# Merged first transfers, products by kind, other banks for one FFT stage and a shared last eviction in a one-core attention and spectral-filter kernel

## The chip, the cores and the metric

The kernel runs on one core of one Trainium2 chip. The metric is the device time of one execution, in microseconds (us). The core has a matrix engine (TensorE, "PE"; its weight loads are listed as "PEld"), a vector engine (VectorE, "DVE"), a scalar engine (ScalarE, "ACT"), GpSimd ("POOL") and SyncE ("SP"), which here only issues transfers. PE writes into eight accumulator banks of 128 x 512 float32 each; DVE and ACT read them. Engines work each in its own order of instructions and wait for one another through semaphores.

## The reference

Two independent halves, side by side in the output of shape (1, 2048, 896). The first is attention with 16 query heads of 28 and one key and value head shared by all of them; the second a spectral filter: a two-dimensional real FFT over 2048 x 448, a product with complex weights, and the inverse.

```python
q = (x @ wq).reshape(B, S, H, Dh).transpose(0, 2, 1, 3)   # S=2048, H=16, Dh=28, D=448
k = x @ wk
v = x @ wv
p = softmax(einsum("bhqd,bkd->bhqk", q, k) * Dh**-0.5)
a = einsum("bhqk,bkd->bhqd", p, v).transpose(0, 2, 1, 3).reshape(B, S, H * Dh) @ wo
X = rfft2(x2, axes=(-2, -1)) * (w_r + 1j * w_i)           # x2: a second (1, 2048, 448) input
b = irfft2(X, s=(S, D), axes=(-2, -1))
out = concatenate([a, b], axis=-1)
```

## The kernel before

*Precision.* Products of the attention's linear maps are made of float32 numbers split in a high and a low part: `xh` and `xl` for the input, `wqh` and `wql` for the weights. Three products (high by high, low weight by high input, high weight by low input) are summed in one bank.

*Phase 1, projections.* The sequence is cut in four column chunks `c` of 512. The outputs (queries of 16 heads, keys and values, 512 rows padded) are four groups `g` of 128. The contraction over 448 is cut in four quarters `j`; the last holds 64 rows, stacked twice so that its high and low parts share one product. `split_w` (L257) and `split_x` (L264) make the parts from tiles called `raw`: ACT casts the weights, DVE subtracts; for chunk 0 the inputs' cast is DVE's, later ACT's. `proj` (L275 to L279) issues the products of one group and quarter, `evac` (L281 to L285) copies a finished bank to `qraw` with ACT and takes its largest absolute value with DVE into `qmx`. Chunk 0 runs quarter by quarter over all four groups (L304 to L309), because its inputs arrive from memory meanwhile; chunks 1 to 3 group by group (L327 on). Twenty products of zeros (L229 to L234) run ahead of the first transfer's landing.

*Input transfers.* SP's queue brings `xa` (the input, transposed) in quarters of 128 x 512 and the weights `wq` in quarters of the same size, alternately, each into a `raw` tile of eight buffers; the first weight quarter comes in two pieces of 128 and 384 columns. POOL's queue brings two small key rows (`krow`) into `kf` at the start (L196, L197).

*The FFT along the width, interleaved.* After six of the twelve groups of chunks 1 to 3 (`places`, L287), one eighth `q` of the second input is worked on: `fft1_load` (L86) brings it in, `fft1_fold` (L95 to L108) adds and subtracts on DVE in ten operations, `fft1_a` (L121) multiplies on PE, ACT copies the result out (L124), `fft1_mm` (L136) multiplies again into banks 6 and 7, and `fft1_out` copies those out, with ACT (L145) for q below 6 and DVE (L147) for 6 and 7, and stores them. All other products of phase 1 take banks 0 to 5 in turn (`spin`).

*Keys and bound.* `fetch` gathers the rows of keys and values from `qraw` into `kf` by transfers; `keys(0)` casts the first half to `ka` with ACT (L206) and subtracts with DVE (`kl`, L210). `key_max` takes the largest key value over the maxima of the first groups (`qm`, L296), and PE spreads it (L299); `terms` and `shift` make from it, per head, a bound on the scores (L216 to L221), and `build_q` (L166) the shifted queries. At the handoff (L369 to L431) the last FFT eighths, 16 small transposes of values (L388), `fft1_mm(6)` (L390) and a branch on the bound (L393, L394) follow one another.

*Phase 2, attention.* For each of the 16 pairs of chunk and group, 16 key blocks, and four heads there is a score product (L810, 1024 in all), an exponential (ACT, L827, with 20 buffers for results), and value products into bank 7 (L840). Between them go the second FFT stages, the filter and the output map `wo` (L739).

*What sets the order.* PE's order is the program's own everywhere. For DVE, ACT, SP and POOL, up to L436, a scheduler places instructions by its own cost model among those whose inputs it expects to be ready. From L436 on all engines follow the program, and there a planner decides it when the kernel is built: a clock per engine (`clk`, L442), a time at which each bank comes free (`free`, L443), queues of fill work (`fill`), `score` (L806), `exps`, `values` (L833) and `first_fill` (L852, the product set `fft1_mm(7)`). A score takes the bank that is free first; `first_fill` comes when no bank is free for the first time.

*The tail.* Four products (L955) add the last group's share to four banks, and `wo_out` copies each out with ACT (L744) and stores it from ACT's queue (L749).

Of the kernel before, what the change touches and what calls it, by code (L numbers as in the profile page):

```python
# [12 lines left out]
F32 = mybir.dt.float32  # L13
# [3 lines left out]
AF = mybir.ActivationFunctionType  # L17
# [5 lines left out]
S, D, H = 2048, 448, 16  # L23
# [10 lines left out]
WARM = 10, 10  # L34
# [3 lines left out]
def kernel(ctx: ExitStack, tc: tile.TileContext, t: dict):  # L38
# [90 lines left out]
    def fft1_mm(q):  # L129
        w = xb[q][1]  # L130
        pb = view(bank[6], 2, 226), view(bank[7], 2, 226)
        for p in range(2):
            a = at1.pop((q, p))
            for h in range(2):
                for e in range(2):
                    mm(pb[h][64 * e:64 * e + 64, p], w[64 * h:64 * h + 64, 2 * p + e], a[64 * h:64 * h + 64, e],  # L136
                       start=True, stop=True)
        return pb
# [48 lines left out]
    with tc.tile_pool(name="f1", bufs=2) as f1[0], tc.tile_pool(name="w1", bufs=1) as w1:  # L187
# [8 lines left out]
        nc.gpsimd.dma_start(kf[DH:DH + 1], t["krow"][0:1])  # L196
        nc.gpsimd.dma_start(kf[32 + DH:64], t["krow"][1:5])  # L197
# [26 lines left out]
        with tc.tile_pool(name="x1", bufs=2) as x1:  # L224
# [11 lines left out]
            def raw(src, eng):  # L236
                r = x1.tile([128, 512], F32, name="raw", bufs=8)
                eng.dma_start(r, src)
                return r


            first = slice(0, 128), slice(128, 512)
            xr, wr = {}, {}
            xr[0, 0] = raw(t["xa"][0, :, 0], nc.sync)
            wr[0] = x1.tile([128, 512], F32, name="raw", bufs=8)
            for s in first:
                nc.sync.dma_start(wr[0][:, s], t["wq"][:, 0, s])
            for j in range(1, NK):
                xr[0, j] = raw(t["xa"][0, :, j], nc.sync)
                wr[j] = raw(t["wq"][:, j], nc.sync)  # L250

# [23 lines left out]
            def proj(pq, xh, xl, g, j):  # L275
                gs = slice(g * 128, (g + 1) * 128)
                parts = ((wqh, xh), (wql, xh), (wqh, xl)) if j < 3 else ((wqh, xh), (wql, xh))
                for n, (w, x) in enumerate(parts):
                    mm(pq, w[:, j, gs], x[:, j], start=(j == 0 and n == 0), stop=(j == 3 and n == 1))  # L279
# [24 lines left out]
            for j in range(NK):  # L304
                split_x(*xs[0], 0, j)
                split_w(j)
                for g in range(NG):
                    proj(pqs[g], *xs[0], g, j)
                xr[1, j] = raw(t["xa"][1, :, j], nc.sync)  # L309
            fft1_consts()  # L310
            fft1_load(0)
            parts_of(1)
            for j in range(NK):
                split_x(*xs[1], 1, j)
                xr[2, j] = raw(t["xa"][2, :, j], nc.sync)
# [11 lines left out]
            for c in range(1, NC):  # L327
                for g in range(NG):
# [4 lines left out]
                    if g == 0 and c < 3:  # L333
                        parts_of(c + 1)
                        for j in range(NK):
                            split_x(*xs[c + 1], c + 1, j)
                            if c < 2:
                                xr[c + 2, j] = raw(t["xa"][c + 2, :, j], nc.sync)
# [51 lines left out]
        pb6 = fft1_mm(6)  # L390
# [52 lines left out]
    free = [0.0] * 6 + [2.0]  # L443
# [297 lines left out]
    def wo_out(p, c, k, on_act=False):  # L741
        if on_act:
            y = pp.tile([128, D], F32, name="yb", tag="p")
            nc.scalar.activation(y, p, AF.Copy)  # L744
        else:
            y = ap.tile([128, D], F32, name="ya")
            V.tensor_copy(y, p)  # L747
        r0 = c * CW + k * 128
        (nc.scalar if on_act else nc.sync).dma_start(t["oa"][r0:r0 + 128], y)  # L749
# [204 lines left out]
    for k in range(4):  # L954
        mm(tail[k], o[:, 128 * k:128 * k + 128], w3, start=False, stop=True)  # L955
        wo_out(tail[k], c, k, True)
# [55 lines left out]
def _layout(A_x, A_wq, A_wk, A_wv, A_wo, B_x, B_w_r, B_w_i):  # L1012
# [3 lines left out]
    z["xa"] = xt.reshape(NK, 128, NC, CW).transpose(2, 1, 0, 3)  # L1016
# [4 lines left out]
    z["wq"] = wq.reshape(D, 512)[rows].reshape(NK, 128, 512).transpose(1, 0, 2)  # L1021
# [51 lines left out]
```

## Time and profile before

| | us |
|---|---|
| Median of 3 runs | 644.1 (643.01 to 645.8) |
| Profiled execution, its own time | 643.85 |
| Profiled execution, span | 642.1 |
| PE busy | 633.9 |
| ACT busy | 548.0 |
| DVE busy | 333.4 |

The span runs from the first to the last instruction or transfer that the profiler saw; the execution's own time is a little longer. Times in rows of the timeline count from the span's start. A row gives start, length, engine, line, operation, output <- inputs and the tile's shape, and in brackets the idle time ahead of it with what ended it; "xN" folds several instructions into one row. Phase 1 lasts until about 72 us, the attention until about 627, the tail until the end.

### The profile page before, as it was taken

The numbers are of one execution on the slowest core, as the hardware profiler recorded it, in microseconds if no ns is written. First come the engines' busy times: TensorE is split into PE (matmuls) and PEld (weight loads), VectorE is DVE, ScalarE is ACT, GpSimd is POOL, SyncE is SP. The second block draws the span as 40 slices with busy tenths as digits, with TensorE's granted clock in tenths as the row PEclk, the third lists the DMA queues.
The fourth block names the chain that finished last, engine by engine and source line by source line (L and its number), as shares of the span: only waits on it lengthen the run. The fifth ranks groups of instructions, "written<-read, shape, count | busy, mean of one in ns | idle before, by whom it ended". The sixth has DMA issues, their size and how long they took to land.

```text
span 642.1 us, 11693 instructions
## 1 busy us (share of the span) xinstructions
PE 633.9 (99%) x4384; PEld 359.1 (56%) x4384; DVE 333.4 (52%) x685; ACT 548.0 (85%) x1101; POOL 91.2 (14%) x170
## 2 busy tenths in 40 slices
PE   8999999999999999999999999999999999999997
PEld 6877544444444455554445655655665665564444
DVE  6999612499898987896821411315323510321003
ACT  4544799999999997889999879878988888889991
POOL 2021031201021201020132020010211101020200
PEclk9999899999999999999999999999999999999999
DMA  8756499512133321131692332232425131131001
GB/s 275 262 150 181 113 241 211 140 26 59 44 100 87 114 67 32 38 76 28 163 240 64 99 78 69 63 79 83 120 77 142 47 81 47 38 90 44 19 1 58
DMA packets 31162, 63.35 MB, mean 99 GB/s; under 512 B 7093, under 2 KB 18918, under 8 KB 29884
## 3 DMA queue, kind: packets, MB, share of 16 engines
q1 hardware_dynamic: 23168, 39.98, 23.3%
q0 software_dynamic: 7360, 21.69, 12.6%
q10 hardware_dynamic: 576, 0.92, 0.4%
q8 instruction: 35, 0.57, 0.4%
q14 instruction: 23, 0.19, 0.1%
HBM read 30.56 MB, written 15.02 MB: 71 GB/s over the span
## 4 chain that ended last, share of the span: by engine, by line
PE 88%; ACT 0%; ACTq 0%; DVE 0%; issue 0%; DVEq 0%
PE b L810 41%; PE b L840 36%; PE b L739 6%; PE b L680 2%; PE b L661 2%; PE b L136 0%; ACT yb L744 0%; ACTq L749 0%; PE b L955 0%; DVE bs L147 0%; ACTq L393 0%; ACT bs L145 0%; DVEq L147 0%; ACTq L744 0%
## 5 line engine op out<-in xcount | busy, mean ns | idle before, releaser
L827 ACT ACTIVATE p<-b 128x512 f32<-128x512 f32 x1024 | 506.6, 777 | 48.1 <-PE b L810 46.9
L810 PE MATMUL b<-qa,ka 128*128 128x512 f32 x1024 | 284.3, 411 | 0.4 <-DVE bs L147 0.4
L810 PEld LDWEIGHTS b<-qa,ka 128*128 128x128 f32 x1024 | 182.7, 189 | 126.0 <-ACT p L827 82.3
L840 PE MATMUL b<-p,vs 128*32 128x512 f32 x2048 | 240.0, 597 | 0.0
L840 PEld LDWEIGHTS b<-p,vs 128*32 128x32 f32 x2048 | 56.5, 109 | 121.7 <-issue 120.3
L710 POOL DMA_DIRECT2D sd<-qraw x15 | 8.8, 589 | 260.0 <-DVE qraw L705 260.0
L705 DVE COPY qraw<-b 128x512 f32<-128x512 f32 x15 | 10.4, 692 | 65.6 <-PE b L840 65.6
L747 DVE COPY ya<-b 128x448 f32<-128x448 f32 x12 | 7.5, 625 | 56.9 <-PE b L739 54.7
L719 POOL DMA_DIRECT2D R<-rd x60 | 29.9, 504 | 42.4 <-DMA rd<-rs 30.3
L544 DVE SCALAR_TENSOR_TENSOR X<-w,X 128x226 f32<-128x226 f32 (+2 forms) x72 | 34.0, 473 | 2.4
L667 DVE COPY X<-b 113x512 f32<-113x512 f32 (+1 forms) x16 | 11.1, 692 | 34.1 <-ACT p L827 28.7
L685 DVE COPY X<-b 128x226 f32<-128x226 f32 x16 | 6.3, 392 | 41.4 <-ACT p L827 38.5
L279 PE MATMUL b<-xh,wqh 128*128 128x512 f32 x64 | 25.8, 403 | 0.9 <-ACT wqh L261 0.9
L283 ACT ACTIVATE qraw<-b 128x512 f32<-128x512 f32 x16 | 9.2, 600 | 19.0 <-PE b L279 19.0
L279 PE MATMUL b<-xh,wql 128*128 128x512 f32 x64 | 25.1, 392 | 0.1
L739 PE MATMUL b<-woh,oh 128*128 128x448 f32 x60 | 22.1, 368 | 0.0
L739 PE MATMUL b<-wol,oh 128*128 128x448 f32 x60 | 22.1, 368 | 0.0
L739 PE MATMUL b<-woh,ol 128*128 128x448 f32 x60 | 22.0, 366 | 0.0
L279 PE MATMUL b<-xl,wqh 128*128 128x512 f32 x48 | 18.8, 391 | 0.0
L727 DVE TENSOR_TENSOR qraw<-qraw,R 128x512 f32<-128x512 f32 x15 | 10.3, 685 | 14.7 <-DMA R<-rd 14.7
L680 PEld LDWEIGHTS b<-cs,X 113*128 113x128 f32 (+1 forms) x128 | 16.8, 191 | 1.4
L537 DVE SCALAR_TENSOR_TENSOR w<-X 128x113 f32<-128x113 f32 (+2 forms) x56 | 17.5, 352 | 0.1
(108 smaller groups left out, 515.9 us busy)
## 6 DMA issues: line engine op xcount, KB each, us to landing
qa<-qa SPq DMA_DIRECT2D x15, 512.0 KB, 4.2
X<-t POOLq DMA_DIRECT2D x16, 452.0 KB, 6.5
wf<-w POOLq DMA_DIRECT2D x10, 452.0 KB, 4.6
raw<-xa SPq DMA_DIRECT2D x16, 256.0 KB, 5.0
xb<-xb SPq DMA_DIRECT2D x8, 512.0 KB, 3.6
qa<-qh SPq DMA_DIRECT2D x60, 64.0 KB, 2.0
qa<-ql SPq DMA_DIRECT2D x60, 64.0 KB, 2.8
R<-rd POOLq DMA_DIRECT2D x60, 64.0 KB, 2.3
```

Source lines behind the costliest of these rows:

```text
L279: mm(pq, w[:, j, gs], x[:, j], start=(j == 0 and n == 0), stop=(j == 3 and n == 1))
L537: STT(out, y, sy, x, op0=ALU.mult, op1=ALU.add if c > 0 else ALU.subtract)
L544: todo(226 * n, lambda d=d, q=q: STT(both(d), t[0].rearrange("p r n f -> p r (n f)"), q, both(a), op0=ALU.mult, op1=ALU.add))
L661: mm(pz[:w, j], c2t[q % 2][:, e, j, :w], fit[q % 2][:, j], start=True, stop=True)
L667: V.tensor_copy(zt[q % 2][e][:w], view(bank[b], 4, 128)[:w].rearrange("p j (r n) -> p r j n", r=2))
L680: mm(py[:, k], z[:w, r, js], fc["cs3"][:w, k], start=True, stop=True)
L705: V.tensor_copy(o, bank[7])
L719: nc.gpsimd.dma_start(R[32 * i:32 * i + 32], rd[i:i + 1].to_broadcast([32, CW]))
L739: mm(p, x[c][:, g, s], w[:, g], start=(g == 0 and n == 0), stop=(g == NG - 1 and n == 2))
L810: mm(bank[b], ka[:, kc * 128:(kc + 1) * 128], qa[c, g][:, h], start=True, stop=True)
L827: nc.scalar.activation(p, bank[b], AF.Exp, scale=SCALE)
L840: mm(bank[7][32 * i:32 * i + 32], vs[:, kc], pt.pop(4 * st + i), start=(kc == 0), stop=(kc == 15))
```

## The change

Five things change.

1. *Transfers.* For chunk 0, each input quarter and weight quarter lie side by side in memory (`xw`, 128 x 1024) and come in one transfer of 512 KB, four in all. For chunks 1 to 3 two quarters share one transfer (`load_x`, at odd quarters). A `raw` tile is 128 x 1024 with four buffers. The two `krow` transfers are issued by SP, behind the constants and the first FFT input, instead of POOL at the start.
2. *Order of products.* Within a group and quarter the low weights come last instead of second. For chunk 0, quarter 0, the products go by kind: four of high by high, four with the low input, four with the low weights.
3. *Warm products.* Sixteen instead of twenty.
4. *Banks.* `fft1_mm(6)` writes the next two of banks 0 to 5 instead of 6 and 7; the planner's starting times of the free banks follow.
5. *Last eviction.* `last_out` replaces ACT's four evictions: quarters 0 and 2 by ACT, quarter 1 by DVE, quarter 3 in two halves of 224 columns by ACT and DVE, each stored from the queue of ACT or SP.

Since the scheduler places the instructions of DVE and ACT in phase 1, their order there differs too, at places whose lines the diff does not touch. The keys' cast (L206) stands on ACT behind the copy-out of chunk 3, group 0, instead of two copy-outs ahead of that. On DVE, two maxima stand ahead of `kl` (L210); `qm` (L296) stands behind fold 5 and both first operations of fold 6, and the first query block ahead of fold 7. On ACT the four copies of L160 stand ahead of the last copy-out of chunk 3. In phase 2 PE begins with 4 scores, `fft1_mm(7)` (16 products on half arrays, two banks), 10 scores and the first values, where it had 8 scores, the set, 6 scores and values; numbers of scores, value blocks and fills stay.

```diff
@@ -31,7 +31,7 @@
 BOUND = float(np.float32(40.0 / SCALE))
 P_BUFS = 20
 LEAD = 7
-WARM = 10, 10
+WARM = 8, 8
 
 
 @with_exitstack
@@ -126,9 +126,9 @@
     def fft1_b(q):
         fft1_out(q, fft1_mm(q))
 
-    def fft1_mm(q):
+    def fft1_mm(q, bs=(6, 7)):
         w = xb[q][1]
-        pb = view(bank[6], 2, 226), view(bank[7], 2, 226)
+        pb = [view(bank[i], 2, 226) for i in bs]
         for p in range(2):
             a = at1.pop((q, p))
             for h in range(2):
@@ -193,8 +193,6 @@
         qmx = w1.tile([128, NG, NC], F32, name="qmx")
 
         nc.gpsimd.memset(kf, 0.0)
-        nc.gpsimd.dma_start(kf[DH:DH + 1], t["krow"][0:1])
-        nc.gpsimd.dma_start(kf[32 + DH:64], t["krow"][1:5])
 
         def fetch(ms, hs, eng=nc.sync):
 
@@ -233,22 +231,20 @@
                 for _ in range(n):
                     mm(nothing[:, :256], idle[:, :128], idle, start=True, stop=True)
 
-            def raw(src, eng):
-                r = x1.tile([128, 512], F32, name="raw", bufs=8)
-                eng.dma_start(r, src)
-                return r
-
+            def raw(src):
+                r = x1.tile([128, 1024], F32, name="raw", bufs=4)
+                nc.sync.dma_start(r, src)
+                return r[:, :512], r[:, 512:]
+
+            def load_x(c, j):
+
+                if j % 2:
+                    xr[c, j - 1], xr[c, j] = raw(t["xa"][c - 1, j // 2])
 
             first = slice(0, 128), slice(128, 512)
             xr, wr = {}, {}
-            xr[0, 0] = raw(t["xa"][0, :, 0], nc.sync)
-            wr[0] = x1.tile([128, 512], F32, name="raw", bufs=8)
-            for s in first:
-                nc.sync.dma_start(wr[0][:, s], t["wq"][:, 0, s])
-            for j in range(1, NK):
-                xr[0, j] = raw(t["xa"][0, :, j], nc.sync)
-                wr[j] = raw(t["wq"][:, j], nc.sync)
-
+            for j in range(NK):
+                xr[0, j], wr[j] = raw(t["xw"][j])
 
             wqh = x1.tile([128, NK, 512], F32R, name="wqh", bufs=1)
             wql = x1.tile([128, NK, 512], F32R, name="wql", bufs=1)
@@ -272,11 +268,12 @@
                 else:
                     nc.vector.tensor_tensor(xh[64:128, j], x[64:128], xh[64:128, j].bitcast(F32), op=ALU.subtract)
 
-            def proj(pq, xh, xl, g, j):
+            def proj(pq, xh, xl, g, j, ns=range(3)):
                 gs = slice(g * 128, (g + 1) * 128)
-                parts = ((wqh, xh), (wql, xh), (wqh, xl)) if j < 3 else ((wqh, xh), (wql, xh))
+                parts = ((wqh, xh), (wqh, xl), (wql, xh)) if j < 3 else ((wqh, xh), (wql, xh))
                 for n, (w, x) in enumerate(parts):
-                    mm(pq, w[:, j, gs], x[:, j], start=(j == 0 and n == 0), stop=(j == 3 and n == 1))
+                    if n in ns:
+                        mm(pq, w[:, j, gs], x[:, j], start=(j == 0 and n == 0), stop=(j == 3 and n == 1))
 
             def evac(c, g, pq):
                 cs = slice(c * CW, (c + 1) * CW)
@@ -304,15 +301,18 @@
             for j in range(NK):
                 split_x(*xs[0], 0, j)
                 split_w(j)
-                for g in range(NG):
-                    proj(pqs[g], *xs[0], g, j)
-                xr[1, j] = raw(t["xa"][1, :, j], nc.sync)
+                for ns in (range(1), range(1, 2), range(2, 3)) if j == 0 else (range(3),):
+                    for g in range(NG):
+                        proj(pqs[g], *xs[0], g, j, ns)
+                load_x(1, j)
             fft1_consts()
             fft1_load(0)
+            nc.sync.dma_start(kf[DH:DH + 1], t["krow"][0:1])
+            nc.sync.dma_start(kf[32 + DH:64], t["krow"][1:5])
             parts_of(1)
             for j in range(NK):
                 split_x(*xs[1], 1, j)
-                xr[2, j] = raw(t["xa"][2, :, j], nc.sync)
+                load_x(2, j)
             for q in range(1, 4):
                 fft1_load(q)
             fft1_fold(0)
@@ -335,7 +335,7 @@
                         for j in range(NK):
                             split_x(*xs[c + 1], c + 1, j)
                             if c < 2:
-                                xr[c + 2, j] = raw(t["xa"][c + 2, :, j], nc.sync)
+                                load_x(c + 2, j)
                     if c == 1 and g == 1:
                         fetch(range(7), halves[0])
                     if c == 3 and g == 1:
@@ -387,7 +387,8 @@
         for b in range(16):
             nc.tensor.transpose(pv[:, b], kf[32:64, b * 128:(b + 1) * 128], ident[32:64, 32:64])
         nc.scalar.activation(vs, pv, AF.Copy)
-        pb6 = fft1_mm(6)
+        six = [next(turn) % 6 for _ in range(2)]
+        pb6 = fft1_mm(6, six)
 
 
         rv = nc.values_load(bits.bitcast(I32)[0:1, 0:1])
@@ -440,7 +441,8 @@
     TT, STT = V.tensor_tensor, V.scalar_tensor_tensor
 
     clk = {"pe": 0.0, "dve": 4.0, "act": 0.0, "mode": "s", "new": False}
-    free = [0.0] * 6 + [2.0]
+    free = [0.0] * 6 + [9.0]
+    free[six[0]], free[six[1]] = 1.6, 2.2
     events, serial = [], count()
     background = deque()
 
@@ -738,15 +740,24 @@
             for n, (x, w) in enumerate(((oh, woh), (ol, woh), (oh, wol))):
                 mm(p, x[c][:, g, s], w[:, g], start=(g == 0 and n == 0), stop=(g == NG - 1 and n == 2))
 
-    def wo_out(p, c, k, on_act=False):
-        if on_act:
-            y = pp.tile([128, D], F32, name="yb", tag="p")
-            nc.scalar.activation(y, p, AF.Copy)
-        else:
-            y = ap.tile([128, D], F32, name="ya")
-            V.tensor_copy(y, p)
+    def wo_out(p, c, k):
+        y = ap.tile([128, D], F32, name="ya")
+        V.tensor_copy(y, p)
         r0 = c * CW + k * 128
-        (nc.scalar if on_act else nc.sync).dma_start(t["oa"][r0:r0 + 128], y)
+        nc.sync.dma_start(t["oa"][r0:r0 + 128], y)
+
+    def last_out(p, k):
+
+        r0 = (NC - 1) * CW + k * 128
+        for n, w in (((0, 224), (224, 224)) if k == 3 else ((k, D),)):
+            s = slice(n, n + w) if k == 3 else slice(0, D)
+            y = pp.tile([128, w], F32, name="yb", tag="p")
+            if n in (0, 2):
+                nc.scalar.activation(y, p[:, s], AF.Copy)
+                nc.scalar.dma_start(t["oa"][r0:r0 + 128, s], y)
+            else:
+                V.tensor_copy(y, p[:, s])
+                nc.sync.dma_start(t["oa"][r0:r0 + 128, s], y)
 
     def w_unit(c, k):
         def go(g):
@@ -953,7 +964,7 @@
         TT(s, s, r, op=ALU.mult)
     for k in range(4):
         mm(tail[k], o[:, 128 * k:128 * k + 128], w3, start=False, stop=True)
-        wo_out(tail[k], c, k, True)
+        last_out(tail[k], k)
 
 
 def _points():
@@ -1013,12 +1024,14 @@
     z = {}
     rows = np.concatenate([np.arange(384), np.tile(np.arange(384, D), 2)])
     xt = np.asarray(A_x)[0].T[rows]
-    z["xa"] = xt.reshape(NK, 128, NC, CW).transpose(2, 1, 0, 3)
+    xt = xt.reshape(NK, 128, NC, CW)
+    z["xa"] = xt[:, :, 1:].reshape(2, 2, 128, NC - 1, CW).transpose(3, 0, 2, 1, 4).reshape(NC - 1, 2, 128, 2 * CW)
     wq = np.zeros((D, H, 32), np.float32)
     wq[:, :, :DH] = np.asarray(A_wq).reshape(D, H, DH)
     kv = np.concatenate([np.asarray(A_wk), np.asarray(A_wv)], 1).reshape(D, 14, 4)
     wq[:, :14, DH:] = kv
-    z["wq"] = wq.reshape(D, 512)[rows].reshape(NK, 128, 512).transpose(1, 0, 2)
+    wq = wq.reshape(D, 512)[rows].reshape(NK, 128, 512)
+    z["xw"] = np.concatenate([xt[:, :, 0], wq], 2)
     wo = np.zeros((H, 32, D), np.float32)
     wo[:, :DH] = np.asarray(A_wo).reshape(H, DH, D)
     z["wo"] = wo.reshape(NG, 128, D).transpose(1, 0, 2)
```

## The prediction

> **What bounds the kernel now.** I read the page first: busy time, the slices, the chain that ended last. Then the timeline of the three places that the change touches (the first 10 us, the stretch from 40 to 84 us, the last 8 us), engine by engine, and a table of windows for the clock.
>
> ```profile
> PE 633.9 (99%) x4384; PEld 359.1 (56%) x4384; DVE 333.4 (52%) x685; ACT 548.0 (85%) x1101; POOL 91.2 (14%) x170
> PEclk9999899999999999999999999999999999999999
> PE 88%; ACT 0%; ACTq 0%; DVE 0%; issue 0%; DVEq 0%
> ```
>
> TensorE (PE) is busy for 99% of the span and carries 88% of the chain; the one dip of its clock is the fifth slice of 16 us. So whatever delays or advances PE's dense sequence in the projections goes through to the end, unless PE was waiting there anyway. The steady part of the attention shows it in two consecutive rows of the chain (start, length, what):
>
> ```profile
> 603.34 1.85 PE b L840 x16
> 605.19 2.04 PE b L810 x8
> ```
>
> 16 value products and 8 scores take 3.89 us, back to back on PE; nothing there takes up a late start. ScalarE's exponentials, one per score, therefore run at 3.89 / 8 = 0.486 us each or faster.
>
> **The front.** First input quarter, first weights, first products:
>
> ```profile
> 1.72 3.70 PE L234 MATMUL b<-idle 128*128 128x256 bf16 x17
> 3.81 0.43 DVE L267 CAST xh<-raw 128x512 fp32r<-128x512 f32 x1 [2.76 <-DMA raw<-xa]
> 3.99 0.31 ACT L261 ACTIVATE wqh<-raw 128x128 fp32r<-128x128 f32 x1 [1.74 <-DMA raw<-wq]
> 5.48 0.39 PE L279 MATMUL b<-xh,wql 128*128 128x512 f32 x1
> 5.71 0.40 PE L279 MATMUL b<-xl,wqh 128*128 128x512 f32 x1
> 6.44 0.52 ACT L261 ACTIVATE wqh<-raw 128x384 fp32r<-128x384 f32 x1 [2.14 <-DMA raw<-wq]
> 7.02 0.50 PE L279 MATMUL b<-xh,wqh 128*128 128x512 f32 x1 [0.91 <-ACT wqh L261]
> 7.78 0.63 ACT L261 ACTIVATE wqh<-raw 128x512 fp32r<-128x512 f32 x1 [0.82 <-DMA raw<-wq]
> 9.59 0.39 PE L279 MATMUL b<-xh,wqh 128*128 128x512 f32 x1
> ```
>
> The other 384 columns of the first weight quarter come only at 6.44, so PE's fourth product waits to 7.02 and the first of quarter 1 starts at 9.59. Two products stand 0.23 us apart (5.48, 5.71). The clock by windows (start:end, length, busy time of PE, PEld, DVE, ACT and POOL with counts, granted clock, DMA share, GB/s):
>
> ```profile
> 5.14:8.56 3.42, 2.42 (x10) 1.49 (x9) 1.55 (x5) 1.15 (x2) 0.00 (x0) 1.00 0.91 303
> 8.56:11.97 3.41, 3.41 (x17) 2.79 (x16) 3.32 (x7) 1.32 (x3) 0.00 (x0) 1.00 1.05 376
> 70.00:73.41 3.41, 2.04 (x19) 1.24 (x20) 1.31 (x3) 1.36 (x4) 0.00 (x0) 1.00 0.25 51
> 73.41:76.83 3.42, 3.42 (x19) 2.12 (x21) 1.65 (x2) 3.42 (x8) 0.00 (x0) 0.50 0.73 172
> ```
>
> *Step 1, merged transfers and products by kind.* The first transfer is now 512 KB instead of 256. At the 376 GB/s of the second window 256 KB more take 0.70 us, so my estimate for its landing is 3.81 + 0.70 = 4.5. The weights' cast (0.63 for 512 columns, row 7.78) is done at about 5.15; then twelve products by kind, 12 x 0.23 = 2.75, end at 7.9 against 9.59: at best -1.7. What limits this is the second transfer. The first megabyte was in only at 7.78 before; if that stays, casts and subtractions of quarter 1 let its first group of products run about 0.35 earlier than before, no more. I take the middle, **-1.0** (ends -1.7 and -0.35). The warm-up's 16 instead of 20 products, 3.70 / 17 = 0.218 us apart, end some 0.9 us earlier, covered by the wait for the transfer; this costs nothing if the clock still rises at 5.14 (price otherwise up to half a window, 1.7, put to the range). The two key-row loads move from POOL's queue to SP's, behind the constants and ahead of the loads of column chunk 2: two issues of 0.43 us (row below), whose products start only after all of chunk 1's; with that cover gone they would cost those 0.9.
>
> ```profile
> 4.04 0.43 SPq L238 DMA_DIRECT2D raw<-xa  x1
> ```
>
> **The order of VectorE and ScalarE in the projections.** This is the largest term. Their order up to 72 us is the scheduler's, not written by hand, and the edits to loads and products change it. In the changed program the cast of the keys `ka` (L206 before) stands on ScalarE behind the copy-out of chunk 3, group 0; before it stood ahead of that. On VectorE, which works in order, the subtraction `kl` (L210) stands behind the two maxima of the newest groups, and behind it fold 4, fold 5 and half of fold 6, and only then `qm`, which the key maximum on PE (L299) needs. The rows of before that price this:
>
> ```profile
> 41.50 1.04 ACT L206 ACTIVATE ka<-kf 32x1024 fp32r<-32x1024 f32 x1
> 47.10 0.60 ACT L283 ACTIVATE qraw<-b 128x512 f32<-128x512 f32 x1 [1.89 <-PE b L279]
> ```
> ```profile
> 43.40 1.20 DVE L210 TENSOR_TENSOR kl<-kf,ka 32x1024 fp32r<-32x1024 f32 x1
> 44.53 1.28 DVE L100 TENSOR_TENSOR f<-xb 113x512 f32<-113x512 f32 x2
> 45.84 0.69 DVE L103 TENSOR_TENSOR xb<-f 113x512 f32<-113x512 f32 x1
> 47.05 0.68 DVE L284 TENSOR_REDUCE qmx<-qraw 128x1 f32<-128x512 f32 x1
> 47.65 0.41 DVE L105 TENSOR_TENSOR f<-xb 113x256 f32<-113x256 f32 x1
> 48.98 0.68 DVE L284 TENSOR_REDUCE qmx<-qraw 128x1 f32<-128x512 f32 x1
> 54.29 0.16 DVE L296 TENSOR_REDUCE qm<-qmx 128x2 f32<-128x8 f32 x1
> ```
> ```profile
> 52.33 1.76 PE L121 MATMUL b<-cs,f 113*32 113x113 f32 x64
> 54.95 0.60 PE L299 MATMUL b<-qm,sel 128*128 128x1 f32 x4
> 66.41 0.39 PE L220 MATMUL b<-prod,blk 128*128 128x12 f32 x2
> ```
>
> The copy-out of chunk 3, group 0 is the row at 47.10. *Step 2.* On before's clock of PE: 47.10 + 0.60, the cast 1.04, `kl` 1.13 (43.40 to 44.53), fold 4's first pair 1.31 (to 45.84), its L103 and L104 1.21 (to 47.05), half of fold 5 0.64, the four quarters L105 to L108 1.42 with the last one's end: 54.45. PE wants fold 4 at 52.33: a stall of 2.1. Then, from the issue-to-issue end at 54.36: half of fold 5 0.64, a maximum 0.60, L103/L104 1.21, half of fold 6 0.64, four quarters 1.33 (47.65 to 48.98), the other half 0.64, `qm` 0.16: 59.6 against 54.95. Together PE is **+4.65** late, the second stall being 2.55. A second way: `kl` starts at 48.74 instead of 43.40, 5.3 late, and VectorE stays full afterwards, so that only its small idle pieces can give something back; ends 4.0 and 5.3.
>
> *Step 3, the clock.* The windows above show a stretch with PE busy for 2.04 of 3.41 us followed by a stretch at 0.50, and one with 2.42 of 3.42 followed by full clock. A stall of 2.1 or 2.55 leaves less than 2.04 in the window that holds most of it. I expect half clock for one window behind the second stall, where PE is again the one to be waited for (the loss behind the first is absorbed by the second stall): half of 3.41, **+1.7** (0 if no window halves, 3.4 if two do on the path).
>
> [...]
>
> *Step 4.* The four copies of L160 now stand on ScalarE ahead of the last copy-out: **+0.4** (0 to 0.6, from such a copy's 0.64 being half of a row of 1.27 for two).
>
> ```profile
> 65.49 1.27 ACT L160 ACTIVATE qa<-ql 32x512 fp32r<-32x512 f32 x2
> ```
>
> **The handoff.** Last PE rows before the attention, and the second block of values:
>
> ```profile
> 70.92 1.42 PE L136 MATMUL b<-a,fw 64*64 64x226 f32 x16 [1.13 <-ACT bs L145]
> 72.79 3.22 PE L810 MATMUL b<-qa,ka 128*128 128x512 f32 x8 [0.45 <-DVE bs L147]
> ```
> ```profile
> 83.08 1.85 PE b L840 x16
> ```
>
> *Step 5, other banks.* Product set 6 waited 1.13 us for ScalarE to empty banks 6 and 7; in its own banks that goes. It also ran for 1.42, with a break for the second bank; without it I take 1.0: together **-1.5** (ends -1.1 and -1.5). Late next is the branch on the bound, which stays.
>
> *Step 6, first scores.* Without that hole PE's window at the handoff stays above the busy share that was followed by half clock, and the first scores run at full rate. By the planner the order is then 4 scores, set 7, 10 scores, values, instead of 8, set 7, 6, values. The second block of values started 83.08 - 72.79 = 10.29 behind the first score; with full clock ScalarE sets it: 16 exponentials x 0.486 = 7.8, and 1.15 for the first score and the last exponential's way: 8.95. **-1.3** (ends -0.6 and -1.35). If steps 2 and 3 put the half clock here instead, this gain is lost and step 3's cost with it.
>
> *Step 7.* Fills and value blocks behind that are as many as before (1024 scores, 98 value blocks); 0, within 0.3.
>
> **The tail.**
>
> ```profile
> 634.37 3.17 PE L955 MATMUL b<-w,qraw 128*128 128x448 f32 x8
> 635.38 0.54 ACT L744 ACTIVATE yb<-b 128x448 f32<-128x448 f32 x1 [6.89 <-PE b L955]
> 638.30 0.54 ACT L744 ACTIVATE yb<-b 128x448 f32<-128x448 f32 x1 [0.41 <-ACT yb L744]
> 638.87 0.34 ACTq L749 DMA_DIRECT2D oa<-yb  x1
> ```
>
> *Step 8.* Four evictions 0.97 apart on ScalarE alone, issues between them, decide the end. Now quarter 1 goes to VectorE, and quarter 3 in halves to both: the last issue comes after PE's last product (about 637.6) and a half eviction, at some 638.4: **-0.5** (ends -0.3 and -0.9).
>
> **Sum.** -1.0 + 4.65 + 1.7 + 0.4 - 1.5 - 1.3 + 0 - 0.5 = +2.4. The profiled execution took 643.85 (span 642.1), 0.25 under the median of 644.1: **646.2 us**.
>
> **Rivals.**
> - [...] 0.20.
> - *VectorE's new order is hidden*: the maxima come early enough, PE runs on, and steps 2 to 4 vanish: 643.85 - 1.0 - 1.5 - 1.3 - 0.5 = 639.6, faster. It decides if fold 4 is in by 52.33 and `qm` by 54.95. Against: 2.1 and 4.65 us of sums of measured rows. 0.10.
> - *Slower: two windows at half clock on the path*, one behind each stall or one more at the handoff, with 1.7 each: 646.2 + 1.7 = 647.9. It decides once PE is still the late engine in the second such window. For it: PE and VectorE are both dense from the key maximum to the row at 66.41, so that little slack takes up a slow window. 0.25.
> - *The merge brings nothing* (the second transfer is as late as before): 0.65 more on any of these; within the forecast's spread.
>
> **How the numbers follow.** The forecast keeps 0.45, of which 0.09 lie above 647.3 by its ends. Half a per cent of 644.1 is 3.2, about what a measurement of this kernel can tell from no change: bounds 640.9 and 647.3. Faster 0.10 (the hidden order), slower 0.25 + 0.09 = 0.34, same 0.56. The range leaves out the hidden order and the upper end of the two windows (649.3 and more): 642.0 to 649.3.
>
> **What would show it.** Right: a wait of PE of about 2 us ahead of set 4's L121 products and of 2.5 ahead of the key maximum, VectorE idle for some 4 to 5 us ahead of `kl`, a clock of 0.50 in a window behind them, no wait ahead of set 6, first product of quarter 1 near 8.6, last store issue near 638.4 on before's clock. Wrong: `kl` running close to 43.4 with VectorE full, or stalls that leave the clock whole, or a second slow window.

## The result, and the profile after

The changed kernel takes 649.9 us (median of 6 runs, 648.69 to 651.94), the kernel before 643.56 (6 runs): a ratio of 1.0096, with a 95% interval of 1.0069 to 1.0123. It is slower by 6.3 us where 2.4 were forecast, beyond the upper end of the range (649.3). The profiled execution is the longest of the six, 651.94 (span 650.1); what it shows at single places is therefore a little more than the median has.

Busy time of the changed kernel, its clock over 40 slices, and its chain:

```profile
PE 637.2 (98%) x4380; PEld 361.2 (56%) x4380; DVE 334.1 (51%) x687; ACT 546.4 (84%) x1100; POOL 89.9 (14%) x168
PEclk9997999998999999999999999999999999999999
PE 84%; DVE 6%; DMA 5%; issue 3%; ACT 1%; POOL 1%; ACTq 0%; SPq 0%; DVEq 0%; POOLq 0%
```

PE's share of the chain falls from 88% to 84%, and VectorE and transfers, which had next to nothing of it before, now stand in it. The clock has two dips: slice 4 (48.8 to 65 us) and slice 10 (146 to 162); before, the one dip was in slice 5 (64 to 80).

In what follows, set `q` is the FFT work on eighth `q`: its first stage is `fft1_a(q)` (L121), its second `fft1_mm(q)` (L136). A value block is 16 value products, one row "x16".

PE's rows at the places of the prediction, in order (start, length, engine, line, what, count, idle time ahead and what ended it):

```profile
8.59 0.39 PE L276 MATMUL b<-xh,wqh 128*128 128x512 f32 x1
52.40 0.38 PE L121 MATMUL b<-cs,f 113*32 113x113 f32 x2 [1.01 <-DVE f L105]
53.07 1.89 PE L121 MATMUL b<-cs,f 113*32 113x113 f32 x62 [0.29 <-DVE f L107]
58.43 1.01 PE L296 MATMUL b<-qm,sel 128*128 128x1 f32 x4 [2.53 <-DVE qm L293]
64.27 1.86 PE L121 MATMUL b<-cs,f 113*32 113x113 f32 x64
76.79 0.99 PE L136 MATMUL b<-a,fw 64*64 64x226 f32 x16
78.25 1.17 PE L821 MATMUL b<-qa,ka 128*128 128x512 f32 x4 [0.46 <-PEq L395]
83.93 1.92 PE L851 MATMUL b<-p,vs 128*32 128x512 f32 x16 [0.51 <-DVE bs L147]
88.07 1.92 PE L851 MATMUL b<-p,vs 128*32 128x512 f32 x16
148.92 2.77 PE L851 MATMUL b<-p,vs 128*32 128x512 f32 x16 [2.16 <-DVE qraw L707]
642.90 3.17 PE L966 MATMUL b<-w,qraw 128*128 128x448 f32 x8
```

Quarter 1 starts 1.00 earlier (8.59 after 9.59), the key maximum 3.48 later (58.43 after 54.95), set 5's first stage 6.13 later (64.27 after 58.14), the first score 5.46 later (78.25 after 72.79). Up to here it is what was forecast, though the last two numbers are larger. At 148.92 a new wait of 2.16 us stands, in a part that was forecast to stay as it was; by the tail (642.90 after 634.37) the loss is 8.5.

The clock, in windows of the length used in the prediction's table, laid so that the clock changes at their edges (start:end, length, busy time of PE, PEld, DVE, ACT, POOL, clock, DMA share, GB/s):

```profile
54.29:57.71 3.42, 1.60 (x43) 0.95 (x34) 3.42 (x9) 2.08 (x4) 0.00 (x0) 1.00 0.94 280
57.71:61.12 3.41, 2.69 (x8) 2.35 (x9) 3.41 (x10) 0.00 (x0) 0.00 (x0) 0.50 0.31 97
61.12:64.53 3.41, 3.41 (x16) 2.24 (x18) 0.12 (x1) 0.15 (x1) 0.00 (x0) 0.50 0.58 142
146.45:149.87 3.42, 1.26 (x14) 0.35 (x16) 3.35 (x7) 3.18 (x7) 0.58 (x1) 1.00 0.16 38
149.87:153.28 3.41, 3.41 (x16) 1.46 (x9) 3.34 (x6) 0.82 (x2) 0.56 (x1) 0.50 0.43 103
```

With each of the two waits the clock falls: at the first for two windows, the fall coming 0.72 us before PE has its key maximum, at the second for one. ScalarE and VectorE at the keys are in the order that was forecast. The cast `ka` stands behind the copy-out of chunk 3, group 0; on VectorE two maxima wait for their copy-outs, then `kl` comes at 47.66 instead of 43.40. That is right behind the end of `ka` (46.59 + 1.04 = 47.63), although the row names a transfer. VectorE's idle time there is 2.5 us in sum, less than the 4 to 5 named as a sign.

```profile
46.10 0.60 ACT L280 ACTIVATE qraw<-b 128x512 f32<-128x512 f32 x1 [1.89 <-PE b L276]
46.59 1.04 ACT L204 ACTIVATE ka<-kf 32x1024 fp32r<-32x1024 f32 x1
```
```profile
44.24 0.69 DVE L281 TENSOR_REDUCE qmx<-qraw 128x1 f32<-128x512 f32 x1 [0.48 <-ACT qraw L280]
46.73 0.69 DVE L281 TENSOR_REDUCE qmx<-qraw 128x1 f32<-128x512 f32 x1 [1.81 <-ACT qraw L280]
47.66 1.21 DVE L208 TENSOR_TENSOR kl<-kf,ka 32x1024 fp32r<-32x1024 f32 x1 [0.25 <-DMA xb<-xb]
```

What made the wait at 148.92? The copy-out of bank 7 on VectorE, which must empty the bank before the next values. VectorE's filter chain ahead of it starts late. Before, first POOL, then VectorE and PE:

```profile
109.48 0.59 POOL L710 DMA_DIRECT2D sd<-qraw  x1 [12.12 <-DVE qraw L705]
114.10 0.56 POOL L711 DMA_DIRECT2D rs<-sd  x1 [4.03 <-DMA sd<-qraw]
114.65 0.51 POOL L487 DMA_DIRECT2D X<-t  x1
```
```profile
121.36 1.10 DVE L502 TENSOR_TENSOR X<-X 128x904 f32<-128x904 f32 x1 [12.17 <-DMA X<-t]
140.36 0.68 DVE L705 COPY qraw<-b 128x512 f32<-128x512 f32 x1
```
```profile
141.65 1.92 PE L840 MATMUL b<-p,vs 128*32 128x512 f32 x16
```

and after:

```profile
114.53 0.59 POOL L712 DMA_DIRECT2D sd<-qraw  x1 [12.08 <-DVE qraw L707]
120.66 0.55 POOL L713 DMA_DIRECT2D rs<-sd  x1 [5.54 <-DMA sd<-qraw]
121.21 0.50 POOL L489 DMA_DIRECT2D X<-t  x1
```
```profile
128.17 1.10 DVE L504 TENSOR_TENSOR X<-X 128x904 f32<-128x904 f32 x1 [13.93 <-DMA X<-t]
145.53 1.09 DVE L526 TENSOR_TENSOR X<-X,w 128x904 f32<-128x904 f32 x1
148.19 0.68 DVE L707 COPY qraw<-b 128x512 f32<-128x512 f32 x1
```

The last of eight loads of `X` stands on POOL's queue behind a small store (`sd`) and its reload (`rs`), which waits for that store. The reload waited 1.5 us longer for the store than before (5.54 after 4.03), so VectorE's chain starts 6.81 later while PE's second value block is only 5.05 later (88.07, before 83.02 in the timeline); and the planner's changed start put one filter operation more (16 instead of 15; the row at 145.53, 1.01 to the next) ahead of the copy-out. 1.76 + 1.01 = 2.77 us late. Before, the copy-out ended at 141.04 and the values began at 141.65, so that 0.61 was to spare: 2.77 - 0.61 = 2.16, the wait measured.

### The profile page after: what moved, and what is told of

It reads as the page before. It is cut to its first block, busy times and chain, and to the rows that moved or that the text cites. A ratio compares the mean times of both kernels' runs of the same rounds, so it can differ in the third digit from the quotient of the medians.

```text
span 650.1 us, 11658 instructions
## 1 busy us (share of the span) xinstructions
PE 637.2 (98%) x4380; PEld 361.2 (56%) x4380; DVE 334.1 (51%) x687; ACT 546.4 (84%) x1100; POOL 89.9 (14%) x168
## 4 chain that ended last, share of the span: by engine, by line
PE 84%; DVE 6%; DMA 5%; issue 3%; ACT 1%; POOL 1%; ACTq 0%; SPq 0%; DVEq 0%; POOLq 0%
PE b L821 35%; PE b L851 31%; PE b L741 6%; PE b L276 5%; PE b L682 2%; PE b L663 2%; PE b L121 1%; DMA wo<-wo 1%; DMA X<-t 1%; DMA t<-bs 1%; DVE X L504 1%; DMA sd<-qraw 1%; DVE X L505 1%; DMA xb<-xb 1%; DMA raw<-xw 1%
```

## The experiments

Times are medians; the ratio is to the kernel before on the same chip, with its 95% interval. "e1" and so on are the labels.

### e1: the key rows back on POOL's queue

```diff
         nc.gpsimd.memset(kf, 0.0)
+        nc.gpsimd.dma_start(kf[DH:DH + 1], t["krow"][0:1])
+        nc.gpsimd.dma_start(kf[32 + DH:64], t["krow"][1:5])
...
-            nc.sync.dma_start(kf[DH:DH + 1], t["krow"][0:1])
-            nc.sync.dma_start(kf[32 + DH:64], t["krow"][1:5])
```

> The changed kernel with the two key-row loads back on POOL's queue at the start, all else as changed. The scheduler then gives VectorE and ScalarE the order of before in the projections. Theory O (that order is what costs): the key maximum on PE stands near 54.95 - 1.0 = 53.9 instead of 58.43, no stall above 1 us ahead of it, no halved clock there, first score near 72.79 - 1.0 - 1.6 = 70.2, time 643.6 - 1.0 - 1.6 - 0.4 - 0.5 = 640.1. Rival P (the 2.2 us stall of PE near 148 us and the slow window behind it come from the planner's new start and not from the late VectorE): they stay, 3.5 more, 643.6. Rival M (the merged transfers delay things by themselves): first score still near 78, time near 650.

Measured: 642.38 us, 0.9977 (0.9958 to 0.9996): 7.5 less than the changed kernel. The order of before is back, and with it PE's rows:

```profile
54.04 0.61 PE L298 MATMUL b<-qm,sel 128*128 128x1 f32 x4
70.27 1.17 PE L821 MATMUL b<-qa,ka 128*128 128x512 f32 x4 [0.46 <-PEq L395]
140.44 1.92 PE L851 MATMUL b<-p,vs 128*32 128x512 f32 x16 [1.63 <-DVE qraw L707]
```

Key maximum and first score stand where theory O put them (53.9 and 70.2). But the wait near 140 is there without the late projections: rival P holds too, in part. The time lies 2.3 above theory O's.

### e2: the key rows on SP's queue, nothing else

```diff
-        nc.gpsimd.dma_start(kf[DH:DH + 1], t["krow"][0:1])
-        nc.gpsimd.dma_start(kf[32 + DH:64], t["krow"][1:5])
...
             fft1_load(0)
+            nc.sync.dma_start(kf[DH:DH + 1], t["krow"][0:1])
+            nc.sync.dma_start(kf[32 + DH:64], t["krow"][1:5])
```

> The kernel before with only the two key-row loads moved to SP, at the place that the change gives them. Theory O: the order of the changed kernel appears, VectorE idles 4 to 5 us ahead of kl, PE waits about 1.3 and 2.5 us, first score 6 to 8 us later than 72.79, time 649 to 652. Rival M: time within 1 us of before, 643.6.

Measured: 651.02 us, 1.0107 (1.0073 to 1.0141). This one edit of the kernel before makes it 6.9 us slower, with the same wait:

```profile
58.24 0.61 PE L297 MATMUL b<-qm,sel 128*128 128x1 f32 x4 [2.53 <-DVE qm L294]
```

So neither the merged transfers nor the order of products flip the scheduler's order; the place of two loads, 40 KB together, in the program does. The loads themselves are not late: in the changed kernel SP issues them at about 10 us, over 30 us before `ka` is cast. Why the scheduler's cost model then orders otherwise is not shown. e2's profile has no wait near 148: all of its loss lies ahead of that.

### e3: the other banks alone

```diff
-        pb6 = fft1_mm(6)
+        six = [next(turn) % 6 for _ in range(2)]
+        pb6 = fft1_mm(6, six)
...
-    free = [0.0] * 6 + [2.0]
+    free = [0.0] * 6 + [9.0]
+    free[six[0]], free[six[1]] = 1.6, 2.2
```

> The kernel before with only the other banks for product set 6 and the planner's starting times. Theory O: first score 72.79 - 1.5 = 71.3, second value block 0.4 to 1.3 earlier still, no stall near 140 us: time 641.5 (640.5 to 642). Rival P: the planner's new VectorE order, one more filter operation (1.02 us) ahead of the third copy-out of bank 7, stalls PE there: 643 to 645.

Measured: 643.16 us, 0.9991 (0.9974 to 1.0008). The first score comes at 70.54. In the profiled execution, the longest of the ten (644.91), the gain is given back at one row, with half clock behind it (142.13 to 145.54):

```profile
141.50 3.09 PE L842 MATMUL b<-p,vs 128*32 128x512 f32 x16 [2.37 <-DVE qraw L707]
```

Rival P. The edit that frees the handoff also changes the planner's start, and with it what stands on VectorE ahead of a copy-out 70 us later.

### e4: merged transfers, products by kind and tail, without banks and key rows

It is e1 with the edit of e3 undone.

> The changed kernel with the key-row loads on POOL and product set 6 in the old banks: merged transfers, products by kind, 16 warm products and the shared last eviction remain. Theory O: 643.6 - 1.0 (front) - 0.5 (tail) = 642.1. Rival P says the same here; rival M says 647 or more.

Measured: 643.13 us, 0.9984 (0.997 to 0.9998), 1.0 less than before. Rival M is out: the merged transfers and the edits that remain with them cost nothing together. Of the 1.5 forecast, two thirds are there. The profile has a wait of 0.76 for the same copy-out at 142.23, with 15 filter operations ahead of it as before the change.

### e5 and e6: the last load of X ahead of the small store

```diff
-        after(18.0 + 2.5 * i, 0.0, spread, i)
+        after(18.0 + 2.0 * i, 0.0, spread, i)
```

on e1 (e5) and on the changed kernel (e6).

> e1 (key rows on POOL's queue, all else as changed) with the last of the eight loads of X, on which VectorE's first filter operation waits, ahead of the small store sd on POOL's queue instead of behind it and its reload (the loads' due times 2.0 instead of 2.5 us apart). Theory Q (the stall of about 2 us near 140 us comes from VectorE starting its filter chain late, because that load waits behind sd): VectorE's first filter operation starts near 112 instead of 119.7, the stall goes, time 642.4 - 1.9 = 640.5 (639.5 to 641). Rival R (one more filter operation ahead of the third copy-out is enough for the stall): it stays, 642.4.

> The changed kernel itself with the same earlier load of X. Theory Q: its stall near 148 (2.2 us) and the slow window behind it go, the loss up to the first score (5 to 6 us) stays: 649.9 - 2.2 to 3.8 = 646 to 647.7. Rival R: 649.9.

Measured: e5 641.43 us, 0.997 (0.9951 to 0.9989); e6 649.39 us, 1.0076 (1.0043 to 1.0109). Neither profile has the wait near 140 or 148 any more, but each has a new one (e6: 1.11 us at 111.00, for the exponentials). In e5, the issues of POOL and SP, and then PE:

```profile
88.64 1.51 POOL L489 DMA_DIRECT2D X<-t  x3
93.31 0.51 SPq L183 DMA_DIRECT2D qa<-qa  x1
93.78 1.95 POOL L489 DMA_DIRECT2D X<-t  x4
```
```profile
104.71 3.27 PE L821 MATMUL b<-qa,ka 128*128 128x512 f32 x7 [2.19 <-DMA qa<-qa]
```

The copy of the next queries (512 KB, issued at 93.31) is in only 11 us later, with the loads of X in flight before and behind it, and PE waits 2.19 us for it. Theory Q was right about the place at 140, and in this execution the edit moved the wait. It is one of the longer of the twelve (644.67); eight took 641.6 or less, and no profile shows whether the wait is in them. e6 gained 0.5 of the 2.2 to 3.8 expected, but its five runs go from 645.26 to 651.68, so that its worth is not settled.

### e7: PE kept busy in its wait

```diff
-                pb = spin(64)
+                full = spin(512)
+                pb = full[:, :64]
+                for _ in range(18):
+                    mm(full[:, 256:512], idle[:, :128], idle, start=True, stop=True)
```

> The changed kernel with 18 products of zeros (256 columns, about 2.0 us at full clock) in PE's order ahead of the key maximum's products, where PE waits 2.5 us. They add work, but only in time in which PE waits. Theory C (the wait itself brings the halved clock, which costs 2.6 us by the trace): the clock stays whole behind the key maximum, group 2 of chunk 3 is back at 0.23 us per product instead of 0.43, first score near 75.6 instead of 78.25, time 647.3. Rival D (PE is not the late engine there, VectorE is): clock whole, first score within 0.7 us of 78.25, time 649.3 or more.

Measured: 647.88 us, 1.0049 (1.0025 to 1.0072), 2.0 less than the changed kernel, by adding work. Its rows:

```profile
54.23 0.38 PE L121 MATMUL b<-cs,f 113*32 113x113 f32 x2 [1.01 <-DVE f L105]
57.66 2.14 PE L297 MATMUL b<-idle 128*128 128x256 bf16 x18
60.25 0.61 PE L299 MATMUL b<-qm,sel 128*128 128x1 f32 x4 [0.46 <-DVE qm L293]
63.42 1.76 PE L121 MATMUL b<-cs,f 113*32 113x113 f32 x64
```

In this execution the front ran 1.8 us later than in the changed kernel's profile (quarter 1 at 10.38 instead of 8.59), so the distances count: from set 4 to set 5 it is 9.19 here and 11.87 there. The halved clock cost 2.7 us, and PE was the late engine: theory C. One pair of profiles would not show that the products of zeros did it, for e12 below keeps the clock whole without them; but all six runs here have a mean clock of 0.997 to 1.000, against 0.991 to 0.997 in the changed kernel's six.

### e8: a place of its own for set 6

e5 with, besides:

```diff
-        bs = fp.tile([128, 2, 2, 2, 113], F32, name="bs")
+        if q == 6:
+            bs = X[:, 0, 0:8].rearrange("p (h u n) f -> p h u n f", h=2, u=2)
+        else:
+            bs = fp.tile([128, 2, 2, 2, 113], F32, name="bs")
```

> e5 and, besides, the copy of product set 6 put into a part of the still empty X instead of one of the two buffers that its successor waits for. Theory: VectorE's copy of set 7 then starts some 1.3 us earlier instead of waiting for a store to land, the first values lose their wait of 0.5 us, the second value block starts 9.0 behind the first score instead of 9.8: 0.5 to 0.8 below e5. Rival: the exponentials set the pace from there, and the 0.5 comes back as a wait for them: equal to e5.

Measured: 643.44 us, 0.9995 (0.9973 to 1.0017), 2.0 above e5 instead of 0.5 to 0.8 below it: a miss in the time, though the runs of the two overlap (640.27 to 647.87 and 639.8 to 646.23). At the place itself it did what was expected. In the changed kernel VectorE's copy of set 7 waits for a store:

```profile
82.71 1.16 DVE L147 COPY bs<-b 128x452 f32<-128x452 f32 x2 [1.84 <-DMA t<-bs]
```

in e8 it follows its predecessor at once, and the second value block starts 9.24 behind the first score (80.90 after 71.66) instead of 9.82. But in the profiled execution (647.1, one of the longest) the wait for the queries' copy that e5 had is there too, 2.94 us long, with half clock from 105.15 to 111.98:

```profile
105.78 3.32 PE L824 MATMUL b<-qa,ka 128*128 128x512 f32 x7 [2.94 <-DMA qa<-qa]
```

The edit was not run on top of e10, so its worth there stays open.

### e9, e10 and e11: which of the two reasons for the late copy-out

e9 is e1 with an earlier due time for the copy-out, e10 e1 with all loads of X behind the fourth of `wo` and ahead of the store, e11 both:

```diff
-                after(clk["pe"] + 0.4, 0.72, group_out, c, g)
+                after(clk["pe"] - 1.2, 0.72, group_out, c, g)
...
-        after(18.0 + 2.5 * i, 0.0, spread, i)
+        after(23.5 + 1.5 * i, 0.0, spread, i)
```

> e1 with the planner's due time for the copy-out of bank 7 1.6 us earlier, so that 15 filter operations instead of 16 stand ahead of the second copy-out on VectorE, as before the change. Theory L (the planner's new order, one operation of 1.02 us more, makes the stall near 140 us): the stall of 1.7 shrinks to 0.7 or less, time 642.4 - 1.0 = 641.4. Rival Q' (the late load of X alone makes it): the stall stays within 0.4 of 1.7, time 642.4.

> e1 with all eight loads of X ahead of the small store sd, as in e5, but behind the fourth load of wo on POOL's queue. Theory: the wait that e5 got near 105 us (VectorE waits for wo's last quarter behind three loads of X, the next queries behind that) is gone, and so is the stall near 140: 642.4 - 1.9 = 640.5. Rival: the loads of X now come later as a whole, VectorE's filter chain starts near 119 again, and the stall stays: 642.4.

> e9 and e10 together. If the late load is the cause, equal to e10 (within 0.5); if the operation more is, equal to e9; if each is half of it, 0.5 to 1 below both.

Measured: e9 641.63 us, 0.9965 (0.995 to 0.998); e10 640.59, 0.995 (0.9933 to 0.9967); e11 641.19, 0.996 (0.9945 to 0.9974). All three profiles are free of the wait near 140. e10, VectorE and then PE:

```profile
116.92 1.10 DVE L504 TENSOR_TENSOR X<-X 128x904 f32<-128x904 f32 x1 [9.34 <-DMA X<-t]
138.57 0.68 DVE L707 COPY qraw<-b 128x512 f32<-128x512 f32 x1
```
```profile
140.05 1.92 PE L851 MATMUL b<-p,vs 128*32 128x512 f32 x16
```

The copy-out ends 0.80 us before the values take the bank; there is no wait, although 16 operations still stand ahead of it. Nor is there one near 105, where e5 had it: the queries' copy is issued at 92.61 and the first load of X at 93.53, behind it. e9's profile, with two loads of X at 87.66 ahead of the copy, does have one, of 1.40 us at 103.30; e1 has the same two loads ahead and no such wait, so that it may come and go with the landing of these transfers. By its time e9 cannot tell the two reasons apart, because in its profile the load of X also landed earlier than in e1 (first filter operation at 116.31 instead of 119.69).

The profiles with the old places of the loads can. The wait should be: how much later the first filter operation comes behind the second value block than before, less the 0.61 that was to spare, plus 1.02 for a 16th operation.

| kernel | first filter operation behind the second value block | operations | sum | wait measured |
|---|---|---|---|---|
| before | 121.36 - 83.02 = 38.34 | 15 | (0.61 to spare) | none |
| changed | 128.17 - 88.07 = 40.10 | 16 | 2.17 | 2.16 |
| e1 | 119.69 - 80.09 = 39.60 | 16 | 1.67 | 1.63 |
| e2 | 128.55 - 89.96 = 38.59 | 15 | (0.36 to spare) | none |
| e3 | 120.75 - 80.44 = 40.31 | 16 | 2.38 | 2.37 |
| e4 | 122.48 - 82.75 = 39.73 | 15 | 0.78 | 0.76 |
| e7 | 126.05 - 86.92 = 39.13 | 16 | 1.20 | 1.21 |

Both reasons count, then. In the changed kernel's profile the late chain alone would give a wait of 1.15 and the operation alone one of 0.41.

e10 has the lowest median of the study: it beats the kernel before by 3.2 us and the changed one by 9.3. e11 is equal to it within their spread.

### e12: the changed kernel with e10's loads

> The changed kernel itself (key rows on SP, slow order in the projections) with the loads of X placed as in e10. Theory: the loss up to the first score stays (first score near 78), the stall of 2.2 us near 148 goes and with it the slow window behind it: 649.9 - 2.2 to 3.8, about 647. Rival (the late VectorE of the projections makes the stall by another way): it stays, 649.9.

Measured: 646.46 us, 1.0043 (1.0028 to 1.0059): 3.4 less than the changed kernel, inside what was expected. The wait of the projections is unchanged, but in this execution the clock stayed whole behind it:

```profile
57.81 0.61 PE L296 MATMUL b<-qm,sel 128*128 128x1 f32 x4 [2.53 <-DVE qm L293]
60.96 1.28 PE L121 MATMUL b<-cs,f 113*32 113x113 f32 x44
```

From set 4 (51.79) to set 5 it is 9.17 us, as in e7. Its ten runs go from 645.13 to 648.8, those at a mean clock of 1.000 below 645.6 and those at 0.993 above 648.2.

## Why the prediction was wrong, point by point

The sizes by experiments: the gains (e10 against before) are 643.75 - 640.59 = 3.2; the order of the projections (e12 against e10, which differ in the place of the key rows alone) costs 646.46 - 640.59 = 5.9; the wait near 148 with what follows it (the changed kernel against e12, which differ in the due time of X alone) 649.9 - 646.46 = 3.4. With each run set against the kernel before on its own chip they are 3.2, 5.5 and 4.0. The three are links of one chain from before to changed, so that they add up to the measured difference by construction; and e10's gain contains the moved loads of X, which are not part of the change. The prediction had gains of 4.3, 6.75 for the order with its clock and copies (steps 2 to 4), and nothing for the third. That 5.9 lies near 6.75 is in part luck: the medians mix executions with and without half clock (step 3).

- *Step 7, fills and value blocks, "0, within 0.3": this step failed.* It counted PE's instructions, found them equal, and took equal counts for equal time. What had moved was VectorE's work: one filter operation ahead of a copy-out, and a load on POOL's queue behind a store that waits for another copy-out. VectorE's share of busy time, 52%, hid that it is full from 121 to 140 us (18.30 of 19.00) and that only 0.61 us was to spare at the copy-out. e3, e10 and e12 show it, and the table above adds it up: 2.2 us in the profile, 3.4 to 4.0 in the medians with the half clock behind it.
- *Step 1, -1.0.* 9.59 to 8.59 in the two profiles, exactly. But over all profiles quarter 1 started at 8.37, 8.96 and 9.59 with single transfers and at 7.98 to 10.38 (eleven profiles, median 8.42) with merged ones, so -1.0 from one pair shows nothing. The landing of the first transfer is not what spreads: in all eleven its first cast starts at 4.24 to 4.95. Eight of them have quarter 1 at 7.98 to 8.69; in e7, e8 and e10 it starts at 9.99 to 10.38, because there the clock rises to full only at 9.36 to 10.23, instead of at 4.91 to 6.65, and products ahead of that rise take longer: in the changed kernel, where it comes at 6.51, the first four take 1.80 us together (from 5.13), the next four 1.08 (from 6.77). That is the price which the prediction put to the range for sixteen instead of twenty products of zeros. The three profiles with twenty all rose by 5.59, but three are too few to show that the four products are the reason. e4's 1.0 for front and tail together is what there is of a gain.
- *Step 2, +4.65 to the key maximum.* Right: 58.43 - 54.95 + 1.0 = 4.48; the second stall was 2.53, forecast 2.55. The first was 1.3 instead of 2.1, because PE's products start on fold 4's first quarter and not on its last. That did not matter, since `qm` sets the end. The rival in which VectorE's new order is hidden falls.
- *Step 3, +1.7.* That half clock behind the second wait can cost time was right (from set 4 to set 5, 11.87 with the wait open and 9.19 with it filled, e7), the size was not, in both directions. Four profiles have the wait of 2.53 left open: from set 4 to set 5 it is 11.87 in the changed kernel and in e6, with two windows at half clock, 10.44 in e2 with one, and 9.17 in e12 with none. So it cost 2.7, 1.3 or 0, and the step had 1.7 for one window. The step's end of 0, without half clock, which has the chance of 0.20, is true of some executions, the rival with two windows of others; but there both stand behind the second wait, and the further one at 149.87 is in none of the rivals.
- *Step 4, +0.4.* Set 5's second stage now starts 72.13 - 70.04 = 2.09 behind set 6's first, before 65.49 - 63.80 = 1.69: 0.4. It also took 1.42 instead of 0.99, which was not forecast, so that the place cost 0.8.
- *Step 5, -1.5.* From the transposes to set 6 it is 76.79 - 75.68 = 1.11 instead of 2.30, and the set takes 0.99 instead of 1.42: -1.6. Right.
- *Step 6, -1.3.* It was -0.4 (9.82 behind the first score instead of 10.23 in the timeline). That the half clock at the handoff goes was right: the three profiles with the old banks have it there (before one window, e2 and e4 two), none of the eleven with the new banks does. But the step looked at the exponentials alone and forgot that the first values need bank 7, which set 7 had filled, and that VectorE's copy of it waits for a store to free its buffer. e8 gives 0.6 of it back at that place; the 9.24 that is left there is still above the 8.95 forecast.
- *Step 8, -0.5.* The last product's end to the span's end was 642.1 - 637.54 = 4.56, now 650.1 - 646.07 = 4.03: -0.5. Right.

That the cover of the two moved loads was SP's queue and cheap was right too (issues of 0.54 and 0.25 us, at 9.76 and 10.34); their cost lay in what the scheduler made of them, which the order in the changed program showed. What no order shows is how far ahead of the late engine the other one stands; for that the trace of before had to be read near 140 us, where it shows 0.61, and was not.

## What to carry to other kernels

Where a planner or scheduler writes the order, compare every engine's order and not only that of the engine that bounds: equal counts on PE say nothing of the engine that must hand it the next bank. VectorE, busy for 52% of the span before, was so for 18.30 of the 19.00 us from 121 to 140, and there an operation or a late load ahead of a hand-over went through to PE as far as it was longer than what was to spare (0.61). On POOL's queue the last load of X stood behind a reload that waited 5.54 us for its own small store. With the loads ahead of that store e10 took 640.59 us where e1 took 642.38; e5, which put three of them ahead of the queries' copy as well, had a wait of 2.19 us for that copy in its profile. So put the large loads that others wait for ahead of a transfer that waits, but not ahead of an earlier need.

## What the runs showed of the hardware

The traces record when the granted clock changed. Before, it rises to full at 5.14, falls to 0.50 at 73.41 and is back at full at 76.83, 3.413 us later. In the changed kernel it rises at 6.51 and falls at 57.71, for 6.83 us, and at 149.87, for 3.41. These falls come 68.27, 51.20 and 143.36 us behind the rise, 20, 15 and 42 times 3.413. The products of zeros begin at 1.10 in both. Why the changes stand at these times was not tested.

In windows of that length, counted from the rise, the same wait of 2.53 us ahead of the key maximum can be compared. In the changed kernel (the rows at 54.29 to 64.53 above) 1.81 us of it lie in one window, PE is busy for 1.60, and the clock falls. Here are e2 and then e12:

```profile
56.49:59.90 3.41, 1.66 (x9) 1.49 (x10) 3.41 (x11) 0.29 (x1) 0.00 (x0) 1.00 0.57 187
```
```profile
53.08:56.49 3.41, 2.20 (x70) 1.55 (x58) 3.41 (x8) 2.08 (x4) 0.00 (x0) 1.00 0.86 270
56.49:59.91 3.42, 2.10 (x11) 1.86 (x12) 3.42 (x10) 0.00 (x0) 0.00 (x0) 1.00 0.46 150
```

In e2 1.75 us lie in one window, and the clock falls at its end; in e12 the wait is split into 1.21 and 1.32, and the clock stays full. So a wait of 2.53 us was followed by 0.50 in the changed kernel and e2, and by full clock in e12.

In none of the windows ahead of the low clock at the key maximum and at the handoff was PE without work: 1.60, 1.66 and 2.04 us of products were in those of the changed kernel, e2 and before. Nor does the busy time alone tell them apart: in e2 the window 73.56:76.97, with 2.28 us of small products, was followed by 0.50, and in e12 56.49:59.91, with 2.10, by full clock. And e7, with the wait filled by products of zeros, is 2.0 us faster than the changed kernel (647.88 after 649.9).
